# Batch 0 in finer pieces, w_tok sorted before its transposes, and batch 0's channel layer ahead of batch 1's attention

## Chip, cores, metric

One core of one Trainium2 chip. The metric is device microseconds (us) of one execution; lower is better. The kernel before: 291.4 us, median of 4 runs (290.9 to 292.0). In the profiled run the time is 1.8 us longer than the span from first to last instruction (292.5 against 290.7 for the kernel before), and positions below are us from the start of the span. Engines: PE is TensorE, DVE VectorE, ACT ScalarE, POOL GpSimd, SP the engine that issues most stores and regroupings.

## What is computed

Two stages, four batches of 768 tokens. Sizes and the parts that matter:

```
q, k, v: (4, 8 heads, 768, 64); 8 blocks of 96 tokens; P = sort_net after 5 rounds of normalising
k_sorted, v_sorted = P mixes the 8 blocks of k and of v          # per head
x = softmax(q_block @ k_sorted_block^T / 8) @ v_sorted_block      # per block, heads side by side: (4, 768, 512)
tok = w_tok @ (alpha1 * x + beta1)                                # 768 x 768, over tokens
u   = x + lam * tok
ch  = relu((alpha2 * u + beta2) @ w_ch1) @ w_ch2                  # 512 -> 2048 -> 512
out = u + lam * ch
```

## The kernel before

Batch 0 is special: nothing can overlap with it from an earlier batch, so its mixes, transposes and attention are written out by hand. From batch 1 on, a batch's attention is mixed with the channel layer (`moe_h` then `moe_ch`) of the batch before. `hf` is a half of the tokens. v of a batch is mixed into `vA`, written to a scratch tensor in HBM (`vscr`) and read back regrouped into `Vs[b % 2]`; attention of batch b cannot multiply by v before this round trip has landed.

```python
def load_weights():                    # POOL queue, in this order
    for g in range(4): pool.dma_start(W1p[... g ...], ...)
    prep_affine()                      # two POOL products: a1lB *= lamB, b1lB *= lamB
    load_raw(1, 1); load_raw(1, 0)     # v and k of batch 1
    for g in range(4): pool.dma_start(W2p[... g ...], ...)
    load_q(1)

def mix_heads(kv, h4, out, copy):      # batch 0: two heads of k or v, one copy of 128x768
    mps = psa([128, 8, 128], FT, "m_ps")
    for t6 in range(6):
        for h2 in range(2): pe.matmul(mps[... t6 ...], raw[:, h, t6, :], bigH[...])
    copy(out..., mps[:, 0:6, :]...)

def prep_wtok(which, eng):             # transposes of w_tok; token rows are 6 x 96 and 6 x 32
    for ks in which:
        pst = psb([128, S], F16, "wtok_ps")
        for tt in range(NT): pe.transpose(pst[0:96, ...],   wt16[:, tt, ks*96:(ks+1)*96], ident16[:])
        for tt in range(NT): pe.transpose(pst[96:128, ...], wt16[:, tt, TAIL+ks*32:TAIL+(ks+1)*32], ident16[:])
        eng(w_tokT[:, ks, :], pst[:])
# ... batch 0's attention (first_attention): pieces of 96 rows; blocks 6 and 7 go to a side
#     tile xs and are gathered from there into rows 96..127 of x by copies on ACT and DVE ...

    emit_attention(0, first_attention)
    # ... token matmuls, u of batch 0, a2T of half 0 ...
    moe_h(0, 0, range(3))
    mix_v(1, 1, range(3, 6), (act.copy,))
    load_raw(2, 1); load_raw(2, 0)     # raw loads of batch 2: as soon as their buffers allow
    mix_k(1)
    moe_h(0, 0, range(3, HT))
    moe_turn(0, 1)
    emit_q(1)
    for b in range(1, B):
        # ... for b > 1: q, raw loads of b + 1, mixes of b ...
        emit_attention(b)              # before the channel layer of b - 1 in the text
        if b > 1: moe_h(b - 1, 0)
        moe_ch(b - 1, 0)
        moe_h(b - 1, 1)
        moe_a(b)                       # token layer of b
        moe_ch(b - 1, 1)
```

The softmax here doesn't subtract the row's maximum and nothing guards it: scores larger than these inputs give would overflow.

## Time and profile before

| | before |
|---|---|
| time, median | 291.4 us |
| PE busy | 267.2 us of a span of 290.7 |
| token matmuls on the whole x of batch 0 start | 42.4 us |
| longest wait of PE | 9.7 us, for batch 1's regrouped v |
| start of batch 2's mixing | 125.15 us, 165.5 us before the end |

Three rows of the page of the kernel before; each digit is a fortieth of the span, in tenths of busy time or of the full clock.

```profile
PE   8689988989509999999999999999999999999992
PEclk9989999999966999999999999999999999999999
DMA  6999999999995973326936124249210133012012
```

A slice is 7.3 us. PE is nearly full, but for a hole in the eleventh and twelfth slices (5 and 0), and the low clock (the two sixes) is in the twelfth and thirteenth, in the hole's end and behind it. The chain of work that ended last names the hole (start, length, what):

```profile
23.53 3.66 PE wtok_ps L65 x48
...
42.40 1.38 PE tok_ps L65 x11
...
56.85 9.95 DMA vscr<-vA
...
67.26 19.11 DMA Vs_98<-vscr
...
86.51 1.46 PE x_ps L65 x16
...
125.15 0.13 PE rep_ps L65
...
184.59 0.13 PE rep_ps L65
```

The round trip of v took 10 + 19 us. All transfers are counted on the core's 16 DMA engines, and raw loads of batches 2 and 3 were in flight beside it. The two rep_ps lines, 59.4 us apart, are the starts of batches 2 and 3. The waits of PE (us in total, times, longest), and the two stretches at the hole:

```profile
PE x_ps L65 <- DMA Vs_98<-vscr: 9.7, 1, 9.7
```

```profile
77.00:86.50 9.50, 0.00 (x0) 0.02 (x1) 0.69 (x1) 0.00 (x0) 1.56 (x1) 0.77 1.99 145
86.50:94.50 8.00, 7.99 (x69) 4.28 (x69) 2.88 (x9) 1.61 (x2) 0.00 (x0) 0.63 0.54 116
```

The columns are the stretch, its length, busy time of PE, weight loads, DVE, ACT and POOL, then the granted clock, the DMA share (packet times added up over the 16 engines; it can pass 1 because packets overlap) and GB/s. PE does nothing for 9.5 us, and the 8 us after it run at a mean clock of 0.63.

### The profile page before, as it was taken

Reading aid. Unit: us, or ns where it says so; the run is one execution under the profiler, and the core shown is the slowest. Engines: PE = TensorE matmul, PEld = TensorE weight load, DVE = VectorE, ACT = ScalarE, POOL = GpSimd, SP = SyncE. Lnnn points to the kernel's source line nnn. Section 1 sums busy time; section 2 is a strip of 40 time slices with the busy share of each in tenths; the row PEclk is TensorE's granted clock in tenths of the full one; section 3 lists DMA queues with packets and bytes.
Section 4 is the critical chain, followed back from the end, with each engine's and each line's share of the span. In section 5 each row is a group of like instructions: output and inputs, shape, how many; then the busy total and the mean of one; then the engine's idle time right before and its main releaser. Section 6 shows DMA issues by size and latency. Waiting matters only on the chain.

```text
span 290.7 us, 5185 instructions
## 1 busy us (share of the span) xinstructions
PE 267.2 (92%) x2068; PEld 149.5 (51%) x2068; DVE 154.8 (53%) x331; ACT 130.2 (45%) x237; POOL 93.7 (32%) x100
## 2 busy tenths in 40 slices
PE   8689988989509999999999999999999999999992
PEld 3467764556214654455456644455466445645541
DVE  6856687833303939757046687670367675023032
ACT  2442497885002664058507631386076322703700
POOL 9517559716500990240042542400423600000000
PEclk9989999999966999999999999999999999999999
DMA  6999999999995973326936124249210133012012
GB/s 87 191 214 241 215 206 206 213 265 209 143 148 115 99 48 62 86 72 137 82 90 106 23 50 98 73 110 108 72 40 2 33 80 97 10 36 72 2 36 72
DMA packets 62263, 30.88 MB, mean 106 GB/s; under 512 B 48856, under 2 KB 57824, under 8 KB 62240
## 3 DMA queue, kind: packets, MB, share of 16 engines
q0 software_dynamic: 23024, 15.60, 36.5%
q1 hardware_dynamic: 39216, 14.96, 28.4%
q8 instruction: 16, 0.26, 0.4%
q14 instruction: 7, 0.06, 0.1%
HBM read 32.78 MB, written 8.65 MB: 143 GB/s over the span
## 4 chain that ended last, share of the span: by engine, by line
PE 71%; DMA 15%; ACT 5%; DVE 3%; POOL 3%; issue 1%; SPq 0%; DVEq 0%; POOLq 0%
PE ch_ps L65 27%; PE h_ps L65 24%; PE tok_ps L65 8%; DMA Vs_98<-vscr 7%; DMA wt_100<-in_moe_w_tok_dram 5%; PE x_ps L65 5%; DMA vscr<-vA 3%; PE sc_ps L65 3%; PE wtok_ps L65 2%; ACT kT L65 2%; POOL qn_82 L65 1%; PE v_ps L65 1%; ACT u_781 L65 1%; ACT vA L65 1%; ACT hTa L65 1%
## 5 line engine op out<-in xcount | busy, mean ns | idle before, releaser
L65 ACT ACTIVATE hTa<-h_ps 128x384 bf16<-128x384 f32 x96 | 45.8, 492 | 69.5 <-PE h_ps L65 68.7
L65 PE MATMUL ch_ps<-W2p,hTa 128*128 128x512 bf16 x288 | 68.7, 386 | 0.0
L65 PEld LDWEIGHTS <-W1p 128*128 128x128 bf16 x512 | 47.7, 98 | 32.4 <-issue 3.3
L65 DVE TENSOR_TENSOR ch_ps<-ch_ps,lamB 128x512 f32<-128x512 f32 x24 | 16.7, 698 | 68.6 <-PE ch_ps L65 64.2
L65 PEld LDWEIGHTS <-hTa 128*128 128x128 bf16 x288 | 28.2, 99 | 33.4 <-issue 1.1
L65 ACT ACTIVATE et<-sc_ps 96x768 f16<-96x768 f32 x32 | 24.6, 805 | 29.7 <-PE sc_ps L65 29.7
L65 PEld LDWEIGHTS <-w_tokT 128*128 128x128 f16 x198 | 16.8, 98 | 16.1 <-issue 1.3
L65 PE MATMUL ch_ps<-W2p,hTb 128*128 128x512 bf16 x96 | 24.8, 379 | 0.0
L65 PEld LDWEIGHTS <-et 96*96 96x96 f16 x256 | 16.4, 129 | 13.7 <-issue 10.5
L65 DVE TENSOR_TENSOR tok_ps<-tok_ps,a1lB 128x512 f32<-128x512 f32 x24 | 16.5, 691 | 11.1 <-PE tok_ps L65 11.1
L65 DVE CAST kT<-k_ps 64x512 f16<-64x512 f32 x24 | 16.5, 689 | 4.3 <-PE k_ps L65 4.0
L65 POOL DMA_DIRECT2D qn<-in_q_dram x12 | 10.7, 910 | 24.0 <-DMA qT<-qn 15.5
L65 DVE RECIPROCAL recip<-x_ps 96x8 f32<-96x8 f32 (+1 forms) x38 | 7.0, 188 | 21.3 <-PE x_ps L65 21.1
L65 PE MATMUL x_ps<-Vs_98,et 96*96 96x65 f16 x128 | 8.5, 216 | 9.7 <-DMA Vs_98<-vscr 9.7
L65 ACT ACTIVATE hTb<-h_ps 128x384 bf16<-128x384 f32 x32 | 15.3, 497 | 3.8 <-PE h_ps L65 3.4
L65 PEld LDWEIGHTS <-hTb 128*128 128x128 bf16 x96 | 9.3, 98 | 10.9
L65 PEld LDWEIGHTS <-kT 64*96 64x96 f16 x256 | 8.7, 124 | 10.9 <-issue 5.7
L65 PE MATMUL h_ps<-a2T_782,W1p 128*128 128x384 bf16 x64 | 11.3, 326 | 2.2 <-ACT hTa L65 1.2
L65 PE MATMUL sc_ps<-qT,kT 64*96 64x96 f16 x256 | 12.3, 217 | 0.2
L65 PE MATMUL h_ps<-a2T_2243,W1p 128*128 128x384 bf16 x64 | 12.2, 327 | 0.1
L65 PE MATMUL h_ps<-a2T_1537,W1p 128*128 128x384 bf16 x64 | 12.2, 327 | 0.1
L65 PE MATMUL h_ps<-a2T_1538,W1p 128*128 128x384 bf16 x64 | 12.1, 326 | 0.0
(265 smaller groups left out, 400.1 us busy)
## 6 DMA issues: line engine op xcount, KB each, us to landing
out_dram<-ost SPq DMA_DIRECT2D x24, 192.0 KB, 2.2
vscr<-vA SPq DMA_DIRECT2D x6, 384.0 KB, 4.6
W1p<-in_moe_w_ch_dram POOLq DMA_DIRECT2D x4, 512.0 KB, 10.5
W2p<-in_moe_w_ch_dram POOLq DMA_DIRECT2D x4, 512.0 KB, 17.2
Vs_98<-vscr SPq DMA_DIRECT2D x4, 384.0 KB, 11.5
qn<-in_q_dram POOLq DMA_DIRECT2D x12, 128.0 KB, 7.9
out_dram<-ost SPq DMA_DIRECT2D x24, 64.0 KB, 2.0
wt_100<-in_moe_w_tok_dram POOLq DMA_DIRECT2D x1, 864.0 KB, 14.7
```

The costliest lines, as they stand in the source:

```text
L65: ins = getattr(self.eng, name)(*args, **kwargs)
```

## The change

The intent: give batch 0 a finer pipeline, and fill the hole with work that is ready. `...` marks cuts.

```diff
+    spin(psb([128, 512], FT, "spin_ps")[:], 7)
     def load_weights():
         for g in range(4):
             pool.dma_start(W1p[...], ...)
-        prep_affine()
         load_raw(1, 1)
-        load_raw(1, 0)
         for g in range(4):
             pool.dma_start(W2p[...], ...)
-        load_q(1)
+            if g == 0:
+                prep_affine()
...
-    def mix_heads(kv, h4, out, copy):            # one 128x768 copy
+    def mix_heads(kv, h4, out):                  # one-bank parts, two engines
+        for lo, hi, copy in ((0, 4, dve.tensor_copy), (4, 6, act.copy)):
+            mps = psb([128, hi - lo, 128], FT, "m_ps")
...
+    def pv_tiles(h4, g, et):                     # attention of batch 0 written into full 128-row tiles
+        xps = bank[:, 0:6 * GRP].rearrange("p (a i g) -> p a i g", i=3, a=2)
+        for rows, cols, i in ((slice(0, BLK), BLK, 0), (slice(BLK, 128), 32, 3)): ...
+        dve.reciprocal(recip[:], xps[:, :, :, D])
+        dve.tensor_tensor(x_of[0][:, 3 * g:3 * g + 3, ...], xps[...], recip[...], ALU.mult)
...
+    def sort_wtok(n):                            # columns of w_tok in the order of the tiles
+        t_ = moep.tile([128, NT, 2, 128], F16, name=f"wtp_{n}", tag="a2T", bufs=3)
+        for lo, hi, base in ((0, 96, 0), (96, 128, TAIL)):
+            dve.tensor_copy(t_[:, :, :, lo:hi], wt16[...])
     def prep_wtok(which, eng):
-                pe.transpose(pst[0:96, ...], wt16[:, tt, ks * 96:(ks + 1) * 96], ident16[:])
-                pe.transpose(pst[96:128, ...], wt16[:, tt, TAIL + ks * 32:...], ident16[:])
+                pe.transpose(pst[:, tt * 128:(tt + 1) * 128], wtp[ks // 2][:, tt, ks % 2, :], ident16[:])
...
+    sc0(2, 0, 1)
+    pv0(1, 0)
+    sort_wtok(0)
+    sc0(2, 1, 1)
+    pv0(1, 1)
+    sort_wtok(1)
+    prep_wtok(range(1), dve.tensor_copy)
...
+    moe_h(0, 0, range(6))
+    mix_v(1, 1, range(4, 6), (dve.tensor_copy,))
+    pool.tensor_copy(gate[:], Vs[1][0:1, 0, 0:2])   # POOL waits for batch 1's v ...
+    load_raw(2, 1)                                  # ... before it loads batch 2
+    load_raw(2, 0)
+    moe_h(0, 0, range(6, HT))
+    moe_turn(0, 1)
+    pe.fixed = True
+    for kk in range(3):                             # channel layer of batch 0 ahead of attention 1
+        moe_ch(0, 0, (kk,))
+        mix_k(1, gs=(kk,))
+        for h4 in ((0,), (1, 2), (3,))[kk]:
+            turn_q(1, h4, dve.tensor_copy)
+    pe.fixed = False
     for b in range(1, B):
...
+            if b == 2:
+                opened = pool.tensor_copy(gate[:], Vs[0][0:1, 0, 0:2])   # a second gate, for batch 3
+                ... load_q(3); load_raw(3, 1); load_raw(3, 0) behind it ...
         emit_attention(b)
         if b > 1:
             moe_h(b - 1, 0)
-        moe_ch(b - 1, 0)
+            moe_ch(b - 1, 0)
```

Smaller parts: k and q of batch 1 are loaded after POOL has added u of batch 0; two of these six adds go to DVE; the last output tile is split into 384 and 128 columns. `spin` multiplies an identity into a PSUM tile that is overwritten later; its only use is to keep PE busy.

More of the change, by code (lines that the diff above doesn't have):

```diff
@@ L143, in load_q, with cross_q @@
             pool.dma_start(qn[:, kt, :, :], q[b].rearrange("h (p kt) d -> kt p h d", kt=NT)[kt])
+        qn_of[b] = qn
+    def cross_q(b):
         with tc.issue_after(regroup[b - 1].ins):
@@ L146, in load_q @@
                 nc.sync.dma_start_transpose(
-                    qT_of[b][:, :, kt, :], qn[:, kt, :, :].rearrange("p h d -> p (h d)")
+                    qT_of[b][:, :, kt, :], qn_of[b][:, kt, :, :].rearrange("p h d -> p (h d)")
                 )
@@ L172 @@
     lamB = const([128, C], FT, "lamB")
+    gate = const([1, 2], F16, "gate")
     ab2 = att.tile([2 * CT, 128], FT, name="ab2", tag="sel", bufs=2)
@@ L349, in mix_v, with mix_k @@
             )
-    def mix_k(b, share=(4, 0, 4)):
+    def mix_k(b, share=(4, 0, 4), gs=range(3)):
         raw = raw_of[(b, 0)]
         rhs = bigP[b][:].rearrange("p g i -> p (g i)")
-        kT = att.tile([128, H4 * NB, BLK], F16, name="kT", tag="kT", bufs=2)
-        kT_of[b] = kT
-        kv_ = kT[:].rearrange("p c (par th tp) -> p th c par tp", th=2, par=2)
-        for g in range(3):
+        if b not in kT_of:
+            kT_of[b] = att.tile([128, H4 * NB, BLK], F16, name="kT", tag="kT", bufs=2)
+        kv_ = kT_of[b][:].rearrange("p c (par th tp) -> p th c par tp", th=2, par=2)
+        for g in gs:
             kps = psa([128, 8, 128], FT, "k_ps")
@@ L371, in mix_k, with mix_k0, mix_v0 @@
                         act.copy(dst, src)
-    def mix_heads(kv, h4, out, copy):
+    def mix_heads(kv, h4, out):
         raw = raw_of[(0, kv)]
-        mps = psa([128, 8, 128], FT, "m_ps")
-        for t6 in range(6):
-            for h2 in range(2):
-                h = 2 * h4 + h2
-                pe.matmul(
-                    mps[h2 * 64:(h2 + 1) * 64, t6, :], raw[:, h, t6, :],
-                    bigH[:, h, :, :].rearrange("p i r -> p (i r)"), start=True, stop=True,
-                )
-        copy(
-            out.rearrange("p i (t r) -> p t i r", r=16),
-            mps[:, 0:6, :].rearrange("p t (i r) -> p t i r", r=16),
-        )
-    def mix_k0(h4, copy):
+        dst = out.rearrange("p i (t r) -> p t i r", r=16)
+        for lo, hi, copy in ((0, 4, dve.tensor_copy), (4, 6, act.copy)):
+            mps = psb([128, hi - lo, 128], FT, "m_ps")
+            for t6 in range(lo, hi):
+                for h2 in range(2):
+                    h = 2 * h4 + h2
+                    pe.matmul(
+                        mps[h2 * 64:(h2 + 1) * 64, t6 - lo, :], raw[:, h, t6, :],
+                        bigH[:, h, :, :].rearrange("p i r -> p (i r)"), start=True, stop=True,
+                    )
+            copy(dst[:, lo:hi], mps[:].rearrange("p t (i r) -> p t i r", r=16))
+    def mix_k0(h4):
         if 0 not in kT_of:
             kT_of[0] = att.tile([128, H4 * NB, BLK], F16, name="kT", tag="kT", bufs=2)
-        mix_heads(0, h4, kT_of[0][:, h4 * NB:(h4 + 1) * NB, :], copy)
+        mix_heads(0, h4, kT_of[0][:, h4 * NB:(h4 + 1) * NB, :])
     vT0 = []
-    def mix_v0(h4, copy):
+    def mix_v0(h4):
         vT0.append(moep.tile([128, NB, BLK], F16, name=f"vT_{h4}", tag="u32", bufs=9))
-        mix_heads(1, h4, vT0[h4][:], copy)
+        mix_heads(1, h4, vT0[h4][:])
     def turn_v0(h4, copy):
@@ L405, in turn_v0, with emit_scores, emit_pv @@
         )
-    def emit_q(b):
-        for h4 in range(H4):
-            turn_q(b, h4, dve.tensor_copy)
     x_of = {}
-    def emit_scores(b, h4):
+    def emit_scores(b, h4, g, spins=0):
         kT = kT_of[b]
         qT = qT_of[b]
-        ets = []
+        blocks = ((0, 1, 2, 6), (3, 4, 5, 7))[g] if b == 0 else range(4 * g, 4 * g + 4)
+        sps = psa([128, 2, 4, 128], FT, "sc_ps")
+        spin(sps[:, 0, :, :].rearrange("p i x -> p (i x)"), spins)
+        for ii, i in enumerate(blocks):
+            for h2 in range(2):
+                rows = slice(h2 * 64, (h2 + 1) * 64)
+                pe.matmul(
+                    sps[0:BLK, h2, ii, 0:BLK], kT[rows, h4 * NB + i, :], qT[rows, h4, :, i * 16:(i + 1) * 16],
+                    start=True, stop=True,
+                )
+        et = att.tile([BLK, 2, 4, BLK], F16, name="et", tag="et", bufs=4)
+        act.activation(
+            et[:].rearrange("p a i (r kt) -> p (a i) r kt", kt=NT),
+            sps[0:BLK].rearrange("p a i x -> p (a i) x")[:, :, 0:BLK].rearrange("p n (kt r) -> p n r kt", kt=NT),
+            AF.Exp, scale=scale,
+        )
+        return et
+    def emit_pv(b, h4, ets, x128, xs):
         for g in range(2):
-            sps = psa([128, 2, 4, 128], FT, "sc_ps")
-            if b == 0:
-                spin(sps[:, 0, :, :].rearrange("p i x -> p (i x)"), 1)
+            xps = psa([BLK, 4, 256], FT, "x_ps")
             for ii in range(4):
@@ L424, in emit_scores @@
                 for h2 in range(2):
-                    rows = slice(h2 * 64, (h2 + 1) * 64)
                     pe.matmul(
-                        sps[0:BLK, h2, ii, 0:BLK], kT[rows, h4 * NB + i, :], qT[rows, h4, :, i * 16:(i + 1) * 16],
-                        start=True, stop=True,
-                    )
-            et = att.tile([BLK, 2, 4, BLK], F16, name="et", tag="et", bufs=4)
-            act.activation(
-                et[:].rearrange("p a i (r kt) -> p (a i) r kt", kt=NT),
-                sps[0:BLK].rearrange("p a i x -> p (a i) x")[:, :, 0:BLK].rearrange("p n (kt r) -> p n r kt", kt=NT),
-                AF.Exp, scale=scale,
-            )
-            ets.append(et)
-        return ets
-    def emit_pv(b, h4, ets, x128, xs, narrow=False):
-        for g in range(4 if narrow else 2):
-            n = 2 if narrow else 4
-            if narrow:
-                bank = psb([128, 4, 128], FT, "x_ps")
-                if narrow > 1:
-                    spin(bank[:].rearrange("p a x -> p (a x)"), narrow - 1)
-                xps = bank[0:BLK].rearrange("p a x -> p (a x)")[:, 0:264].rearrange("p (i x) -> p i x", i=2)
-            else:
-                xps = psa([BLK, n, 256], FT, "x_ps")
-            for ii in range(n):
-                i = n * g + ii
-                for h2 in range(2):
-                    pe.matmul(
-                        xps[:, ii, h2 * GRP:h2 * GRP + D + 1], ets[i // 4][:, h2, i % 4, :],
+                        xps[:, ii, h2 * GRP:h2 * GRP + D + 1], ets[g][:, h2, ii, :],
                         Vs[b % NV][:, (2 * h4 + h2) * NB + i, 0:D + 1],
@@ L456, in emit_pv @@
                     )
-            recip = att.tile([BLK, n, 2], FT, name="recip", tag="recip", bufs=3)
+            recip = att.tile([BLK, 4, 2], FT, name="recip", tag="recip", bufs=3)
             sums = xps[:, :, D:D + GRP + 1:GRP]
@@ L460, in emit_pv @@
             dve.reciprocal(recip[:], sums)
-            for lo, hi in ((0, n),) if narrow or g == 0 else ((0, 2), (2, 4)):
-                i = n * g + lo
+            for lo, hi in ((0, 4),) if g == 0 else ((0, 2), (2, 4)):
+                i = 4 * g + lo
                 cols = slice(h4 * 128, (h4 + 1) * 128)
@@ L468, in emit_pv, with emit_attention @@
                 )
-    def emit_attention(b, between=None):
+    def pv_tiles(h4, g, et):
+        bank = psb([128, 4, 128], FT, "x_ps")[:].rearrange("p a x -> p (a x)")
+        xps = bank[:, 0:6 * GRP].rearrange("p (a i g) -> p a i g", i=3, a=2)
+        for rows, cols, i in ((slice(0, BLK), BLK, 0), (slice(BLK, 128), 32, 3)):
+            for h2 in range(2):
+                for ii in range(3):
+                    vi = 3 * g + ii if i == 0 else 6 + g
+                    lhsT = et[:, h2, ii, :] if i == 0 else et[:, h2, 3, 32 * ii:32 * ii + 32]
+                    pe.matmul(
+                        xps[rows, h2, ii, 0:D + 1], lhsT, Vs[0][:, (2 * h4 + h2) * NB + vi, 0:D + 1],
+                        start=True, stop=True,
+                    )
+        recip = att.tile([128, 2, 3], FT, name="recip", tag="recip0", bufs=3)
+        dve.reciprocal(recip[:], xps[:, :, :, D])
+        dve.tensor_tensor(
+            x_of[0][:, 3 * g:3 * g + 3, h4 * 128:(h4 + 1) * 128].rearrange("p i (a d) -> p a i d", d=D),
+            xps[:, :, :, 0:D], recip[:].unsqueeze(3).to_broadcast([128, 2, 3, D]), ALU.mult,
+        )
+    def emit_attention(b):
         x128 = moep.tile([128, NT, C], F16, name="x128", tag="x128", bufs=2)
@@ L473, in emit_attention, with gather @@
         x_of[b] = x128
-        def gather(lo, hi, copies=(dve.tensor_copy,) * 3):
+        def gather(lo, hi):
             for a in range(3):
-                copies[a](x128[96:128, a:a + 4:3, lo:hi], xs[32 * a:32 * a + 32, :, lo:hi])
-        def pv(h4, ets):
-            emit_pv(b, h4, ets, x128, xs, narrow=2 if between and h4 < H4 - 1 else 0)
-        if between:
-            between(pv, gather)
-            return
-        prev = emit_scores(b, 0)
+                dve.tensor_copy(x128[96:128, a:a + 4:3, lo:hi], xs[32 * a:32 * a + 32, :, lo:hi])
+        prev = [emit_scores(b, 0, g) for g in range(2)]
         for h4 in range(1, H4):
-            cur = emit_scores(b, h4)
-            pv(h4 - 1, prev)
+            cur = [emit_scores(b, h4, g) for g in range(2)]
+            emit_pv(b, h4 - 1, prev, x128, xs)
             prev = cur
@@ L491, in emit_attention @@
                 gather(0, 384)
-        pv(H4 - 1, prev)
+        emit_pv(b, H4 - 1, prev, x128, xs)
         gather(384, C)
@@ L497 @@
     rs = const([128, NT], FT, "rs")
+    wtp = []
+    def sort_wtok(n):
+        t_ = moep.tile([128, NT, 2, 128], F16, name=f"wtp_{n}", tag="a2T", bufs=3)
+        wtp.append(t_)
+        for lo, hi, base in ((0, 96, 0), (96, 128, TAIL)):
+            w = hi - lo
+            dve.tensor_copy(
+                t_[:, :, :, lo:hi],
+                wt16[:, :, base + 2 * n * w:base + (2 * n + 2) * w].rearrange("p t (k c) -> p t k c", c=w),
+            )
     def prep_wtok(which, eng):
@@ L502, in prep_wtok @@
             for tt in range(NT):
-                pe.transpose(
-                    pst[0:96, tt * 128:(tt + 1) * 128], wt16[:, tt, ks * 96:(ks + 1) * 96], ident16[:],
-                )
-            for tt in range(NT):
-                pe.transpose(
-                    pst[96:128, tt * 128:(tt + 1) * 128],
-                    wt16[:, tt, TAIL + ks * 32:TAIL + (ks + 1) * 32], ident16[:],
-                )
+                pe.transpose(pst[:, tt * 128:(tt + 1) * 128], wtp[ks // 2][:, tt, ks % 2, :], ident16[:])
             eng(w_tokT[:, ks, :], pst[:])
@@ L554, with tok_part @@
     tok_of = {}
-    def tok_part(b, kt, lo, hi):
-        if (b, kt) not in tok_of:
-            if b == 0 and kt >= 3:
-                pair = psa([128, 2, C], FT, "tok_ps")
-                for n in range(2):
-                    tok_of[(b, kt + n)] = pair[:, n, :]
-            else:
-                tok_of[(b, kt)] = psb([128, C], FT, "tok_ps")[:]
+    def tok_part(b, kt):
+        if b == 0 and kt == 3:
+            pair = psa([128, 2, C], FT, "tok_ps")
+            for n in range(2):
+                tok_of[(b, kt + n)] = pair[:, n, :]
+        elif (b, kt) not in tok_of:
+            tok_of[(b, kt)] = psb([128, C], FT, "tok_ps")[:]
         for ks in range(NT):
             pe.matmul(
-                tok_of[(b, kt)][:, lo:hi], w_tokT[:, ks, kt * 128:(kt + 1) * 128],
-                x_of[b][:, ks, lo:hi], start=(ks == 0), stop=(ks == NT - 1),
+                tok_of[(b, kt)], w_tokT[:, ks, kt * 128:(kt + 1) * 128],
+                x_of[b][:, ks, :], start=(ks == 0), stop=(ks == NT - 1),
             )
@@ L574, in moe_tok @@
                 if not done:
-                    tok_part(b, kts[n], 0, C)
+                    tok_part(b, kts[n])
                 tps = tok_of[(b, kts[n])]
@@ L637, in moe_h, with moe_ch @@
             act.activation(hT_of[(b, hf)][m], hps[:], AF.Relu)
-    def moe_ch(b, hf):
+    def moe_ch(b, hf, kks=range(3)):
         hT = hT_of[(b, hf)]
-        for kk in range(3):
+        for kk in kks:
             kt = 3 * hf + kk
-            cps = psb([128, C], FT, "ch_ps")
-            for m in range(HT):
-                pe.matmul(
-                    cps[:], hT[m][:, kk * 128:(kk + 1) * 128], W2p[:, m, :],
-                    start=(m == 0), stop=(m == HT - 1),
-                )
-            ost = att.tile([128, C], FT, name="ost", tag="ost", bufs=2)
-            dve.tensor_tensor(cps[:], cps[:], lamB[:], ALU.mult)
-            dve.tensor_tensor(ost[:], cps[:], u_of[b][kt][:], ALU.add)
-            nc.sync.dma_start(out[b, kt * 96:(kt + 1) * 96, :], ost[0:96, :])
-            nc.sync.dma_start(out[b, TAIL + kt * 32:TAIL + (kt + 1) * 32, :], ost[96:128, :])
+            last = b == B - 1 and kt == NT - 1
+            ost = att.tile([128, C], FT, name="ost", tag="ost", bufs=2)
+            for lo, hi in ((0, 384), (384, C)) if last else ((0, C),):
+                cps = psb([128, hi - lo], FT, "ch_ps")
+                for m in range(HT):
+                    pe.matmul(
+                        cps[:], hT[m][:, kk * 128:(kk + 1) * 128], W2p[:, m, lo:hi],
+                        start=(m == 0), stop=(m == HT - 1),
+                    )
+                dve.tensor_tensor(cps[:], cps[:], lamB[:, lo:hi], ALU.mult)
+                dve.tensor_tensor(ost[:, lo:hi], cps[:], u_of[b][kt][:, lo:hi], ALU.add)
+                nc.sync.dma_start(out[b, kt * 96:(kt + 1) * 96, lo:hi], ost[0:96, lo:hi])
+                nc.sync.dma_start(out[b, TAIL + kt * 32:TAIL + (kt + 1) * 32, lo:hi], ost[96:128, lo:hi])
@@ L656, with sc0, pv0 @@
+    ets = {}
+    def sc0(h4, g, spins=0):
+        ets[(h4, g)] = emit_scores(0, h4, g, spins)
+    def pv0(h4, g):
+        pv_tiles(h4, g, ets[(h4, g)])
+    x_of[0] = moep.tile([128, NT, C], F16, name="x128", tag="x128", bufs=2)
     mixing_heads()
     turn_q(0, 2, act.copy)
-    for h4 in range(H4):
-        mix_v0(h4, act.copy if h4 == 3 else dve.tensor_copy)
-        if h4 == 0:
-            turn_q(0, 3, act.copy)
+    mix_v0(0)
+    turn_q(0, 3, act.copy)
+    for h4 in range(1, H4):
+        mix_v0(h4)
@@ L662 @@
     load_weights()
-    mix_k0(0, act.copy)
+    mixing_matrices(1)
     turn_v0(0, dve.tensor_copy)
-    mix_k0(1, dve.tensor_copy)
-    def first_attention(pv, gather):
-        e0 = emit_scores(0, 0)
-        turn_v0(1, dve.tensor_copy)
-        turn_v0(2, dve.tensor_copy)
-        e1 = emit_scores(0, 1)
-        turn_v0(3, dve.tensor_copy)
-        prep_wtok(range(4), dve.tensor_copy)
-        mix_k0(2, dve.tensor_copy)
-        mix_k0(3, dve.tensor_copy)
-        prep_wtok(range(4, 6), act.copy)
-        pv(0, e0)
-        e2 = emit_scores(0, 2)
-        prep_rs()
-        prep_ab2()
-        pv(1, e1)
-        e3 = emit_scores(0, 3)
-        pv(2, e2)
-        gather(0, 256, (act.copy,) * 3)
-        moe_start(0)
-        moe_row(range(2))
-        pv(3, e3)
-        gather(256, C, (act.copy, act.copy, dve.tensor_copy))
-        for kt in range(3):
-            tok_part(0, kt, 0, 256)
-        mixing_matrices(1)
-        moe_row(range(2, NT))
@@ L694 @@
-    emit_attention(0, first_attention)
-    for kt in range(3):
-        tok_part(0, kt, 256, C)
-    for kt in range(NT):
-        moe_add(0, kt)
-    moe_tok(0, range(3), done=True)
-    for kt in range(3, NT):
-        tok_part(0, kt, 0, C)
-        mix_v(1, 1, range(kt - 3, kt - 2), (act.copy,))
+    mix_k0(0)
+    mix_k0(1)
+    turn_v0(1, dve.tensor_copy)
+    sc0(0, 0, 2)
+    sc0(0, 1, 2)
+    mix_k0(2)
+    turn_v0(2, dve.tensor_copy)
+    sc0(1, 0, 1)
+    pv0(0, 0)
+    sc0(1, 1, 1)
@@ new lines @@
+    pv0(0, 1)
+    mix_k0(3)
+    turn_v0(3, dve.tensor_copy)
+    sc0(2, 0, 1)
[5 more added lines that the diff above has]
+    prep_wtok(range(1), dve.tensor_copy)
+    sc0(3, 0)
+    pv0(2, 0)
+    prep_wtok(range(1, 2), dve.tensor_copy)
+    sort_wtok(2)
+    sc0(3, 1)
+    pv0(2, 1)
+    prep_wtok(range(2, 4), act.copy)
+    pv0(3, 0)
+    prep_wtok(range(4, 5), dve.tensor_copy)
+    prep_wtok(range(5, 6), act.copy)
+    pv0(3, 1)
+    prep_ab2()
+    prep_rs()
@@ L703 @@
+    moe_start(0)
+    moe_row(range(2, NT))
+    for kt in range(2, NT):
+        moe_add(0, kt)
+    load_raw(1, 0)
+    load_q(1)
+    for kt in range(2):
+        dve.scalar_tensor_tensor(
+            u_of[0][kt][:], b1lB[:], rs[:, kt:kt + 1], x_of[0][:, kt, :], op0=ALU.mult, op1=ALU.add
+        )
+    moe_tok(0, range(3))
+    tok_part(0, 3)
+    tok_part(0, 4)
     moe_turn(0, 0)
+    tok_part(0, 5)
+    mix_v(1, 1, range(0, 4), (dve.tensor_copy, act.copy))
     pe.fixed = act.fixed = False
-    turned = act.last
+    order = [pe.last, act.last]
@@ L709 @@
     stack = ExitStack()
-    stack.enter_context(tc.issue_after(turned.ins))
-    moe_h(0, 0, range(3))
-    mix_v(1, 1, range(3, 6), (act.copy,))
+    for eng in order:
+        stack.enter_context(tc.issue_after(eng.ins))
+    moe_h(0, 0, range(6))
+    mix_v(1, 1, range(4, 6), (dve.tensor_copy,))
+    pool.tensor_copy(gate[:], Vs[1][0:1, 0, 0:2])
     load_raw(2, 1)
@@ L715 @@
     pool.fixed = False
-    mix_k(1)
-    moe_h(0, 0, range(3, HT))
+    moe_h(0, 0, range(6, HT))
     moe_turn(0, 1)
     stack.close()
-    emit_q(1)
+    pe.fixed = True
[5 more added lines that the diff above has]
+    pe.fixed = False
     for b in range(1, B):
         if b > 1:
-            load_q(b)
-            if b + 1 < B:
-                load_raw(b + 1, 1)
-                load_raw(b + 1, 0)
+            if b > 2:
+                cross_q(b)
             mixing_matrices(b)
             mix_v(b)
+            if b == 2:
+                opened = pool.tensor_copy(gate[:], Vs[0][0:1, 0, 0:2])
+                with tc.issue_after(opened.ins):
+                    load_q(3)
+                    load_raw(3, 1)
+                    load_raw(3, 0)
             mix_k(b)
@@ L736 @@
         moe_ch(b - 1, 1)
+        if b == 1:
+            load_q(2)
+            cross_q(2)
     for hf in range(2):
```

## The prediction

> **What bounds the kernel.** The page gives PE 267.2 us busy of 290.7. In the table of stretches PE is nearly full from 95 us on, one batch every 59.4 us (rep_ps at 125.15 and 184.59 in the chain of waits). After the start of batch 2's mixing (125.15) 165.5 us follow, all PE work. What is not PE-bound lies before:
> - 0 to 44 us, batch 0. Token matmuls that need the whole x start at 42.4. w_tok lands at 23.4; then PE, DVE and ACT take turns: 72 half-width w_tok transposes (5.5 us), mixes copied by one engine (0.96 us each), x in 96-row pieces, gather copies (ACT 0.62 us each).
> - 49 to 59 us: about 2.3 us of PE waits on ACT.
> - 76.8 to 86.5 us: PE waits 9.7 us for batch 1's regrouped v (Vs_98<-vscr). vscr<-vA took 9.95 us and Vs_98<-vscr 19.1 us, beside raw loads of batches 2 and 3; in later batches the pair took about 5 and 6 to 9 us. After the gap the granted clock is 0.5 to 0.76 until 95, another 3 us. (Trainium skill, "TensorE: Matmul & The Clock Gate", Part 1: an idle window halves the clock; the trace agrees.)
>
> **The change, costed.**
> 1. Channel layers first: PE does h(0,0), 10.4 us, ch(0,0), 10.36, batch 1's k mix, 1.4, and q turns, 2.0, before attention 1 needs Vs_98. The raw loads of batches 2 and 3 are gated, so vscr and regroup should take about 5 + 8 us. vA done at about 52, Vs_98 at 65 to 68, needed at about 72: the 9.7 us stall and 3 us of slow clock go.
> 2. Batch 0: mixes in one-bank parts, DVE 128x512 (0.69) beside ACT 128x256 (about 0.4). Attention into full tiles: eight times recip (0.18) and a 128x384 multiply (about 0.55), 5.9 us, against 9.1 us plus six gather copies. Sorting w_tok adds six DVE copies; here 32x512 f16 took 0.285 and 32x768 0.353 us, about four elements a cycle (Trainium skill, "VectorE: DVE Perf Modes", perf-mode tier table, agrees), so 2.1 us in all; transposes fall from 72 to 36 (saves about 1.8 us of PE).
>  DVE now limits the front: from bigH (13.6 us) v mixes 2.8 (PE-paced, to 17.5), mixing_matrices(1) 2.5, k mixes and Vs copies 5.5, attention 5.9, sorts 2.1, w_tokT 1.7, plus waits: x whole at about 36.5.
> 3. Two of six moe_adds move to DVE; token matmuls run unsplit, 7.8 us; h(0,0) starts at about 46.5, not 50.6.
>
> **Sum.** h start 46.5; h, two turns, v parts: 59; ch, k mix, q turns: 72.5; scores and pv 5.3, h(0,1) 10.4, tok(1) 7.8, ch(0,1) 10.4: 106.5 (before 125.15). Plus 165.5, less 0.7 for the split last tile: 271.3. I add 1.5 us for unseen waits: **273 us**, range 268 to 280. Faster by over 2%: 0.94; within 2%: 0.05; slower: 0.01.
>
> **What would show it.** No Vs_98 wait in the chain; vscr and Vs_98 landings near 5 and 8 us; no slice with clock below 0.9 after 25 us; PE continuous from about 46 us; tok start near 36.5; DVE the busiest engine from 14 to 37; later batches unchanged at 59.4 us.
>
> **What would make it wrong.** Vs_98 later than 72 us (k and q loads of batch 1 still queued): PE would stall and lose its clock. DVE front slower than summed (sort copies not in the fast mode, POOL contention: 32x256 gathers went from 0.22 to 1.1 us). POOL blocked at the gate, so batch 1's u rows, or q of batch 2, arrive late. ACT crowded between 43 and 52.

## The result

282.3 us (median of 4 runs, 279.9 to 283.4), against 291.4: the ratio is 0.9675, with a 95% interval of 0.961 to 0.974. A ratio is the mean time of one kernel's fast runs over that of the other's in the same rounds, so not quite the ratio of the medians. The change is faster by about 3%. The predicted 273 us, with 268 to 280, was too low by 9 us.

The rows of the page after the change:

```profile
PE   8889599999999799999999999999999999999993
PEclk9999758999999999999999999999999999999999
DMA  6999999979999905469999143399210242012012
```

The hole in slices 11 and 12 and its slow clock are gone. A new, smaller hole stands in the fifth slice (the 5), where PE was 0.9 busy before, with a clock of 0.7, 0.5 and 0.8 in slices 5 to 7. The chain after the change:

```profile
27.16 4.18 DVE wtp_580 L65 x2
31.39 0.82 PE wtok_ps L65 x6
...
41.90 7.88 PE tok_ps L65 x30
...
53.22 3.90 PE h_ps L65 x24
...
64.72 3.45 PE ch_ps L65 x16
...
78.75 2.04 PE h_ps L65 x11
...
98.20 7.50 PE tok_ps L65 x34
105.70 10.36 PE ch_ps L65 x48
116.06 0.86 PE v_ps L65 x4
```

No Vs_98 in it: its two halves took 7.5 and 9.1 us from issues at 63.8 and 64.2, and attention 1 first reads it at 84.8. In its place stands the first sort of w_tok. The waits of PE now, and the two stretches around the new hole:

```profile
PE wtok_ps L65 <- DVE wtp_580 L65: 3.7, 1, 3.7
PE tok_ps L65 <- DVE x_1203 L65: 1.4, 2, 0.8
```

```profile
24.70:31.40 6.70, 3.03 (x51) 2.18 (x50) 6.42 (x8) 1.98 (x3) 6.70 (x9) 0.97 1.24 209
31.40:43.50 12.10, 12.10 (x142) 9.76 (x143) 7.74 (x19) 5.55 (x10) 1.85 (x3) 0.50 1.18 208
```

For 12.1 us after the wait PE is counted as busy throughout and runs at half clock. What made the sort slow? The groups of DVE by shape in the stretch from 26 to 37 us (the last columns are total us and mean ns):

```profile
L65 DVE COPY wtp_580<-wt_100 128x1152 f16<-128x1152 f16 x1 | 3.7, 3711 | 0.0
...
L65 DVE COPY wtp_657<-wt_100 128x1152 f16<-128x1152 f16 x1 | 0.5, 451 | 0.0
L65 DVE COPY wtp_611<-wt_100 128x1152 f16<-128x1152 f16 x1 | 0.5, 450 | 0.0
```

Three copies of one shape: 3711, 450 and 451 ns. The timeline of all engines at the first one:

```profile
26.14 1.12 POOL L65 DMA_DIRECT2D raw_346<-in_v_dram  x2
...
27.16 4.17 DVE L65 COPY wtp_580<-wt_100 128x1152 f16<-128x1152 f16 x2
27.21 0.82 POOL L65 DMA_DIRECT2D W2p<-in_moe_w_ch_dram  x1
28.00 1.33 POOL L65 TENSOR_TENSOR a1lB<-a1lB,lamB 128x512 f32<-128x512 f32 x1
29.23 1.31 POOL L65 TENSOR_TENSOR b1lB<-b1lB,lamB 128x512 f32<-128x512 f32 x1
30.44 2.31 POOL L65 DMA_DIRECT2D W2p<-in_moe_w_ch_dram  x3
```

The two copies of the pair are merged in the DVE line; the first lasts 3.71 us, so it ends at 30.87. POOL was never idle from 26.1, and its two products, which the change moved to this place, end at 30.54, a third of a microsecond before. The copy is of the kind that the prediction put at about four elements a cycle. The Trainium skill, page "SBUF — State Buffer", section "Who interferes with whom", says that such copies use a pair of SBUF ports that DVE shares with POOL, and that the one that comes second "fully blocks". That is the theory that the experiments test. Rivals: the first copy is slow in itself, by its strided halves or by the DMA traffic of 209 GB/s; or POOL's descriptor writing blocks it, and not the products.

### The profile page after: what moved, and what is told of

It is laid out like the page before. It is cut to its first block, busy times and chain, and to the rows that moved or that the text cites. A ratio compares the mean times of both kernels' runs of the same rounds, so it can differ in the third digit from the quotient of the medians.

```text
span 280.5 us, 5152 instructions
## 1 busy us (share of the span) xinstructions
PE 266.7 (95%) x2057; PEld 149.2 (53%) x2057; DVE 160.1 (57%) x332; ACT 126.1 (45%) x233; POOL 92.1 (33%) x100
## 4 chain that ended last, share of the span: by engine, by line
PE 85%; DVE 8%; ACT 4%; issue 1%; DMA 1%; DVEq 0%
PE ch_ps L65 29%; PE h_ps L65 27%; PE tok_ps L65 11%; PE x_ps L65 5%; PE sc_ps L65 4%; ACT kT L65 2%; PE wtok_ps L65 2%; DVE wtp_580 L65 1%; DVE x_1203 L65 1%; PE v_ps L65 1%; PE k_ps L65 1%; PE q_ps L65 1%; PE m_ps L65 1%; ACT et L65 1%; PE vt_ps L65 1%
## 5 line engine op out<-in xcount | busy, mean ns | idle before, releaser
L65 ACT ACTIVATE hTa<-h_ps 128x384 bf16<-128x384 f32 x96 | 46.1, 493 | 52.3 <-PE h_ps L65 51.4
L65 PE MATMUL ch_ps<-W2p,hTa 128*128 128x512 bf16 (+2 forms) x300 | 66.6, 371 | 0.0
L65 DVE TENSOR_TENSOR ch_ps<-ch_ps,lamB 128x512 f32<-128x512 f32 (+2 forms) x25 | 16.9, 675 | 63.8 <-PE ch_ps L65 61.1
L65 PEld LDWEIGHTS <-w_tokT 128*128 128x128 f16 x180 | 15.2, 101 | 18.9 <-issue 2.9
L65 PE MATMUL ch_ps<-W2p,hTb 128*128 128x512 bf16 (+2 forms) x100 | 25.0, 370 | 0.0
L65 PEld LDWEIGHTS <-et 96*96 96x96 f16 (+1 forms) x288 | 17.5, 128 | 3.5 <-issue 0.4
L65 DVE RECIPROCAL recip<-x_ps 96x8 f32<-96x8 f32 (+1 forms) x32 | 6.2, 196 | 14.5 <-PE x_ps L65 14.1
L65 PE MATMUL h_ps<-a2T_800,W1p 128*128 128x384 bf16 x64 | 12.9, 327 | 0.0
L65 PE MATMUL h_ps<-a2T_2219,W1p 128*128 128x384 bf16 x64 | 12.2, 327 | 0.1
L65 PE MATMUL h_ps<-a2T_2220,W1p 128*128 128x384 bf16 x64 | 12.1, 326 | 0.0
L65 PE MATMUL h_ps<-a2T_1504,W1p 128*128 128x384 bf16 x64 | 11.7, 327 | 0.0
L65 PE MATMUL h_ps<-a2T_1505,W1p 128*128 128x384 bf16 x64 | 11.6, 326 | 0.0
L65 PE MATMUL x_ps<-Vs_96,et 96*96 96x65 f16 (+1 forms) x160 | 11.4, 222 | 0.0
```

Of the source, the lines that this page charges most:

```text
L65: ins = getattr(self.eng, name)(*args, **kwargs)
```

## The experiments

Eleven kernels, all correct, in three sets. Each set shared its runs of the kernel before (291.4, 292.2, 292.2 us medians). Times are medians of all 4 runs; ratios are to the kernel before. The changed kernel was not run again in these sets, and the kernel before differed by 0.8 us between them, so a difference of about 1 us from the changed kernel says nothing. Three of the 44 runs were over 1.5% above the fastest of their kernel (the profiled one of the first experiment, 279.65 us, among them); such runs are classed slow and are not in the ratios.

| kernel | us | ratio | clocks of the 4 runs |
|---|---|---|---|
| changed | 282.3 | 0.968 | 0.966 to 0.986 |
| POOL products later | 275.9 | 0.945 | 0.975 to 1.0 |
| first sort on ACT | 278.2 | 0.953 | 0.982 to 0.994 |
| spins in the wait | 277.4 | 0.951 | 0.997 to 1.0 |
| products later and spins | 275.5 | 0.944 | 0.992 to 1.0 |
| no sort | 276.5 | 0.946 | 0.996 to 1.0 |
| batch 0 of before, rest changed | 283.3 | 0.973 | 0.984 to 0.992 |
| batch 0 changed, rest of before | 294.2 | 1.005 | 0.948 to 0.969 |
| no gates | 287.6 | 0.983 | 0.958 to 0.975 |
| gates, channel layer not ahead | 279.6 | 0.957 | 0.978 to 0.987 |
| one row held for attention 1 | 278.0 | 0.952 | 0.973 to 0.985 |
| products later, spins, row held | 273.4 | 0.935 | 0.999 to 1.0 |

### The cause of the slow sort

**POOL products later.** They wait for a part of w_tokT:

```diff
-            if g == 0:
-                prep_affine()
...
     prep_wtok(range(2, 4), act.copy)
+    pool.tensor_copy(gate[:], w_tokT[0:1, 2, 0:2])
+    prep_affine()
     pv0(3, 0)
```

> Edit: only the two GpSimd products (a1lB, b1lB) move, from beside the first w_tok sort copy to behind w_tokT part 2. My theory (the 128x1152 sort copy took 3.71 us, against 0.45 for its twins, because GpSimd held the shared SBUF ports with the two products): the copy falls to at most 1.5 us, PE's wait of 3.67 us for wtp to at most 1.3, the clock no longer drops to 0.5 between 31 and 43 us, the token matmuls start at 36 to 37.5 instead of 41.8, time 5 to 6.5 us below the changed kernel. Rival 1 (the copy is slow by itself, its first use or its strided halves, or because of the DMA traffic of 206 GB/s): it stays at 3.5 us or more and so does the time. Rival 2 (descriptor writing by GpSimd blocks it as well): 2 to 3 us, time 2 us lower.

DVE and then POOL in the profiled run (which was one of the slow runs, 279.65 us; the copy's length is DVE's and POOL's matter, not the clock of PE):

```profile
27.14 1.30 DVE L65 COPY wtp<-wt 128x1152 f16<-128x1152 f16 x2
```

```profile
25.72 1.12 POOL L65 DMA_DIRECT2D raw<-in_v_dram  x2
26.78 1.58 POOL L65 DMA_DIRECT2D W2p<-in_moe_w_ch_dram  x2
...
34.86 1.25 POOL L65 TENSOR_TENSOR a1lB<-a1lB,lamB 128x512 f32<-128x512 f32 x1
```

The pair falls from 4.2 us to 1.3 with descriptor writing still beside it, and PE waits 0.8 us for it instead of 3.7. So the products were the cause of most of it; rival 1 is out, and of rival 2 about 0.7 us is left in this run (1.3 against the 0.6 of an undisturbed pair). In the changed kernel rival 2 has a part too: at its own 0.45 us the copy would have ended at 27.6, but the first product began only at 28.00, and until then POOL was writing descriptors. The time fell by 6.4 us (medians of all four runs). One part of what was expected failed: in this run the clock still fell, as the stretches show, without a wait of that length.

```profile
25.00:30.00 5.00, 4.20 (x65) 3.05 (x63) 4.68 (x11) 1.85 (x4) 4.10 (x6) 0.87 1.23 205
30.00:35.00 5.00, 5.00 (x57) 4.33 (x57) 3.01 (x8) 2.56 (x4) 1.03 (x3) 0.50 1.26 211
35.00:40.00 5.00, 5.00 (x71) 3.89 (x70) 2.82 (x7) 2.29 (x6) 2.35 (x3) 0.50 1.08 207
```

The same program had a clock of 1.0 in two of its four runs (274.2 and 274.5 us), and 0.986 and 0.975 in the others (277.3 and 279.7). So a wait of 3.7 us is not needed for the clock to fall; what decides it in this stretch stays open (see the end of the next chapter).

**First sort on ACT.** ACT has its own ports by the same page.

```diff
-    sort_wtok(0)
+    sort_wtok(0, act.copy)
```

> Edit: only the first sort pair goes to ACT, which was idle 27.97 to 32.8. My theory (ports shared by DVE and GpSimd): the pair takes about 1.7 us on ACT, undisturbed by GpSimd; PE waits under 1.5 us for wtp, the clock stays at 1, token matmuls start at 36.5 to 38, time 4 to 6 us below the changed kernel; the DVE copies of the second sort now meet GpSimd's products instead and may take 1 to 2.5 us. Rival (slow source or DMA traffic): the ACT copy is slow too, 3 us or more, and nothing is gained.

The pair took 1.14 + 0.51 us on ACT beside POOL's work, and PE waited 0.45 us for it: the strided source is not slow to read in itself. The second pair, on DVE, then met the products, as expected, and PE waited 1.1 us for what stood behind it. DVE, then POOL:

```profile
28.35 3.21 DVE L65 COPY wtp<-wt 128x1152 f16<-128x1152 f16 x2
```

```profile
28.25 1.29 POOL L65 TENSOR_TENSOR a1lB<-a1lB,lamB 128x512 f32<-128x512 f32 x1
29.48 1.28 POOL L65 TENSOR_TENSOR b1lB<-b1lB,lamB 128x512 f32<-128x512 f32 x1
```

Its first copy took 2.74 us, so it ended at 31.09, 0.33 us after the second product (30.76). In the changed kernel the same distance was 0.33, and in the next experiment, where again the second pair was hit (3.08 us from 28.45), it was 0.33. Three more experiments below show the same 0.33: the one with a row held at the first pair (3.43 us), and "no gates" and "gates, channel layer not ahead" at the second (2.87 us each, while their first pair took its normal 0.62). These two have the front of the changed kernel, word for word, so which pair is hit depends on small shifts in POOL's queue, and neither the first use nor the place of a copy makes it slow. Whichever copy meets the products ends right behind them: the cause is settled. Time 278.2, 4.0 us below the changed kernel.

**Spins in the wait.** Nothing else is edited.

```diff
     sort_wtok(1)
+    spin(psb([128, 512], FT, "spin_ps")[:], 17)
     prep_wtok(range(1), dve.tensor_copy)
```

> Edit: 17 idle 512-column matmuls fill PE's wait for the first sorted w_tok; the slow copy stays. If the loss is mostly the clock that the wait costs (12 us at 0.5): copy still 3.7 us, clock 1.0 from 31 to 43, token matmuls start at 37.5 to 39 instead of 41.8, time 3 to 4.5 us lower. If the loss is the wait itself: time within 1 us of the changed kernel.

The first w_tok transpose started at 31.3, as late as in the changed kernel (31.4), but the token matmuls at 38.2 instead of 41.8, and all four runs lie between 277.2 and 277.4 with a clock of 0.997 or more. So 4.9 us of the loss was the slow clock: here the transposes start as late as in the changed kernel, but at full clock. The gain is in kind what was expected (3 to 4.5 us), and slightly more. But the copy was not the expected 3.7 us. In the profiled run the products missed the first pair and hit the second, and the late start comes from the spins themselves (DVE, then PE):

```profile
27.15 0.66 DVE L65 COPY wtp<-wt 128x1152 f16<-128x1152 f16 x2
...
28.45 3.56 DVE L65 COPY wtp<-wt 128x1152 f16<-128x1152 f16 x2
```

```profile
27.64 3.84 PE L65 MATMUL spin_ps<-ident 128*128 128x512 f16 x17
```

PE has no listed wait for a sort copy in this run. So it measures a late start at full clock; it does not measure the slow first copy at full clock.

**Both mends:** the products later, and nine spins (six before the first w_tok transposes, one and two before the last two scores of batch 0).

> The two mends together: GpSimd's products moved behind w_tokT as in the first experiment, and nine idle matmuls around the sort (six before the first w_tok transposes, one and two before the last scores). Both losses are then gone: sort copy at most 1.5 us, clock 1.0 from 20 to 60 us in every run, token matmuls start at 35.5 to 37, time 272.5 to 275, and all runs within 1 us of each other (the first experiment's ranged from 274.2 with a clock of 1.0 to 279.7 with 0.975). If the clock falls for another reason than a lack of array work, the spread stays.

275.5 us, runs 275.3 to 276.3: the spread is gone, as expected, the median 0.5 us above the expected range. The two stretches that were shown for the changed kernel:

```profile
24.70:31.40 6.70, 6.70 (x93) 4.37 (x92) 5.33 (x15) 2.68 (x4) 4.85 (x7) 1.00 1.23 206
31.40:43.50 12.10, 12.10 (x149) 8.07 (x149) 8.90 (x18) 8.04 (x14) 9.47 (x9) 1.00 1.18 209
```

The token matmuls start at 36.2 and h(0,0) at 46.1; the prediction had 36.5 and 46.5. The spins are not free: the two runs with the products later and without spins that kept their clock were 1.0 to 1.3 us faster than this median.

**No sort.** The changed kernel with the 72 half-width transposes of before.

```diff
-    sort_wtok(0)      # and (1), (2)
-                pe.transpose(pst[:, ...], wtp[ks // 2][:, tt, ks % 2, :], ident16[:])
+                pe.transpose(pst[0:96, ...], wt16[...], ident16[:])       # and 96:128
```

> The changed kernel without the sort: 72 half-width transposes straight from the loaded w_tok, no sort copies on DVE. If the sort costs more than it saves as the change placed it: no wait for wtp, clock 1.0 from 25 to 45 us, token matmuls start at 37 to 39 instead of 41.8, time 276 to 279. If sorting is worth its price even so: time at or above the changed kernel's 282.

276.5 us, four runs within 0.3, token matmuls at 37.3: as expected, 5.7 us faster than the changed kernel. As the change placed it, the sort cost far more than it saved. Without disturbance it may be worth 1 to 2 us (275.5 with both mends, 274.2 and 274.5 in the two full-clock runs with the products later, against 276.5); these kernels differ in more than the sort, and the intervals of the first pair overlap, so that is not shown.

### Which part brought the gain

**Batch 0 of before, the rest changed.** Built from the kernel before: its batch 0, with the changed order of loads, gates and channel layer.

> Batch 0 as before the change (no sorting, wide mixes, narrow attention pieces), everything from the first channel layer on as after it. My theory: the whole gain comes from the new order behind batch 0 (no wait for Vs_98, no slow clock), and the new batch 0 costs time as it stands: h(0,0) starts at 49 to 51 us against 53.2, time 278 to 281, 1 to 4 us below the changed kernel. Rival (the finer batch 0 carries a good part of the gain): time 285 or more.

283.3 us: between the two expected ranges, so neither is right as stated. The part behind batch 0 alone brings 8.1 of the 9.1 us. So the finer batch 0 is worth about 1 us as the change placed it, which is within the noise; mended, it is worth almost 8 (275.5 with both mends against 283.3). This kernel has small waits of its own: h(0,0) starts at 51.4 us, PE waits 1.0 us there for a2T, and 1.6 us more for batch 2's v mix around 117 us.

**Batch 0 changed, the rest of before.** The changed kernel with the old order of loads, no gates, and attention 1 ahead of the channel layer.

> Batch 0 as changed (sorted w_tok, finer mixes), everything from the first channel layer on as before the change: attention 1 ahead of the channel layer, raw loads of batches 2 and 3 not held back. My theory (the whole gain comes from the order behind batch 0): PE again waits 8 to 14 us for Vs_98 and its clock falls after it, time 288 to 294, within 2% of the kernel before. Rival (the finer batch 0 carries half the gain): 284 to 287.

294.2 us, no gain, but not for the reason I gave: PE waited only 2.0 us for the regrouped v. It waited 6.6 us for k of batch 1, which the scheduler had put ahead of batch 0's transposes in PE's order, and v itself was mixed only by 67 us. Its sort was hit as well (PE waited 3.0 us for it). The combination brought a wait of its own, so it shows that the finer batch 0, as it stood, gains nothing in the old surroundings, and says little of why.

**No gates.**

```diff
-    pool.tensor_copy(gate[:], Vs[1][0:1, 0, 0:2])
...
-                opened = pool.tensor_copy(gate[:], Vs[0][0:1, 0, 0:2])
-                with tc.issue_after(opened.ins):
+                (the three loads of batch 3 ungated)
```

> The changed kernel with both GpSimd gates removed, so that raw loads of batches 2 and 3 and q of batch 3 start as soon as their buffers allow. If the gates matter: the regroup into Vs_98 takes 15 us or more again, lands later than 84.8 us, where attention 1 first reads it, and PE waits; time 2 us or more above the changed kernel. If the order alone is enough: Vs_98 lands before 84.8 even beside these loads (before the change the pair took 29 us from 57, that is 86 here), PE waits at most 2 us and the time is within 2 us.

287.6 us, or 286.7 for the three fast runs (the fourth, 294.3, is a slow one): by the ratios, 0.983 against 0.968, about 4.5 us above the changed kernel. The gates matter, but again the wait is another than expected: Vs_98 took up to 14.7 us and still landed in time, at 79.7 before the first read at 87.3. The loss is 4.8 us in which PE waits for a PSUM tile that DVE cannot empty, because its store buffers are held by output stores, and a clock of 0.65 and 0.67 from 80 to 85 and to 90 us. The last of these stores took 5.8 us to land; the first was issued only at 72.1, because issuing the regroup ahead of it took SP 7.1 us instead of 2.1. A long landing alone is not enough: in the changed kernel two stores took 7.9 and 8.8 us and PE did not wait. Lastly, there are 1.9 us in which u of batch 1 waits for POOL, busy with loading q.

**Gates, channel layer not ahead.**

```diff
-        moe_ch(0, 0, (kk,))
...
         emit_attention(b)
         if b > 1:
             moe_h(b - 1, 0)
-            moe_ch(b - 1, 0)
+        moe_ch(b - 1, 0)
```

> The changed kernel with the gates and its order of loads kept, but ch(0,0) emitted after attention 1 again, as before the change. If the gates alone had removed the wait (Vs_98 landed by 71.8 us in the changed kernel, and without ch(0,0) PE would first read it at about 70): PE waits at most 2 us for it, time within 1.5 us of the changed kernel. If the order of PE is needed too: a wait of 3 us or more for Vs_98, slow clock behind it, time 3 us or more above.

279.6 us, with no wait of PE for Vs_98 at all; it reads it first at 77.3. So putting the whole channel layer ahead was not needed to close the hole. The gates were not needed for it either: without them, with the channel layer ahead, no wait for Vs_98 came (the experiment before this one). Either was enough; k and q of batch 1 loaded late are common to both and were not tested alone. The time is 2.6 us below the changed kernel, though the intervals of the two ratios overlap; part of that is the next point (h(0,1) is followed by no wait for x here), part the clock of the sort stretch, which differs from run to run.

**One row held for attention 1.** After attention 1, PE of the changed kernel waits 1.4 us for x of batch 1: h(0,1) is used up by then.

```diff
     for kk in range(3):
-        moe_ch(0, 0, (kk,))
+        if kk < 2:
+            moe_ch(0, 0, (kk,))
...
         if b > 1:
             moe_h(b - 1, 0)
             moe_ch(b - 1, 0)
+        else:
+            moe_ch(0, 0, (2,))
```

> The changed kernel with the third output row of ch(0,0) emitted after attention 1 and no longer fixed in PE's order. My theory (the 1.4 us that PE waits for x of batch 1 before its token matmuls come from a lack of other work, h(0,1) being used up): the wait goes, time 1 to 2 us lower. Rival (the scheduler puts the row elsewhere, or DVE, which copies the gathered rows, is what limits there): same within 0.5 us.

278.0 us, 4.3 lower, more than the 1 to 2 expected. The token matmuls of batch 1 run without a gap (PE's timeline):

```profile
88.53 5.37 PE L65 MATMUL h_ps<-a2T,W1p 128*128 128x384 bf16 x32
93.73 7.93 PE L65 MATMUL tok_ps<-x,w_tokT 128*128 128x512 f16 x36
```

From the start of h(0,0) to the end of ch(0,1) it takes 60.6 us (51.3 to 111.9) instead of 62.8 (53.1 to 115.9), so the row is worth 2.2 us. The other 2 us lie before h(0,0), where nothing was edited: the clock of the sort stretch again (low for 10.2 us in this profile, 13.7 in that of the changed kernel).

**All together:** products later, spins, row held.

> Mended changed kernel (GpSimd products later, nine idle matmuls) with, in addition, the third row of ch(0,0) kept back for attention 1. If the two gains add (275.5 less the 1.4 us that PE waits for x of batch 1): 273.5 to 274.5, no PE wait over 0.5 us between 20 and 110 us, clock 1.0. If they don't: 275 to 276.

273.4 us, all four runs between 273.3 and 273.5, as expected. No wait of PE over 0.3 us is listed after 20 us, and the page shows a full clock:

```profile
PE   8889999999999999999999999999999999999993
PEclk9999999999999999999999999999999999999999
```

It beats both kernels: 0.935 of the kernel before, 8.9 us below the changed one.

## Why the prediction was wrong

The sum of the prediction, boundary by boundary (us from the start of the span; starts from PE's timeline and the chain):

| boundary | predicted | changed | both mends | mends and row |
|---|---|---|---|---|
| token matmuls of batch 0 start | 36.5 | 41.8 | 36.2 | 36.3 |
| h(0,0) starts | 46.5 | 53.1 | 46.1 | 46.2 |
| ch(0,0), k mix and q turns end | 72.5 | 78.7 | 71.7 | in other order |
| ch(0,1) ends | 106.5 | 116 | 108.9 | 106.9 |
| span ends | 271.3 | 280.5 | 273.5 | 271.7 |

**The step that failed** is in the second item of the costs: "2.1 us in all" for the six sort copies, and with it "x whole at about 36.5" and "no slice with clock below 0.9 after 25 us". The copies took 5.9 us (3.71 + 0.54, 0.45 + 0.52, 0.45 + 0.25). The copy rate was right: 0.45 us for 1152 elements, twice, as the tier table of the Trainium skill's page "VectorE: DVE Perf Modes" and this trace had it. What I left out was POOL. The text named the danger ("POOL contention: 32x256 gathers went from 0.22 to 1.1 us") but no term of the sum carried it, though the diff shows the two products moving to exactly this place in POOL's queue. The delay of 3.6 us at the first pair became 6.6 us at the start of h(0,0), because it came with more than 12 us of half clock; the spins experiment, with the transposes starting as late, got 4.9 us back.

**The second, smaller miss:** from 72.5 to 106.5 I added up scores, products, h(0,1), tok(1) and ch(0,1) as if PE were never short of work: 34.0 us. It took 37.3 in the changed kernel (78.7 to 116), and 37.2 with both mends. Attention's own latency needs more filling than h(0,1) has: 1.4 us is the wait for x of batch 1, and holding back one row of ch(0,0) recovered 2.2 us. Most of the rest is a term that was set too low: scores and products with h(0,1) kept PE from 78.7 to 95.9, which leaves them about 6.8 us beside h's 10.4, not 5.3.

**Right in outcome, other in cause:** the wait for Vs_98 and the slow clock behind it went, as predicted, and the two transfers took about 5 and 8 to 9 us as predicted. The headline "channel layers first" is not shown to have done it: with the gates and the order of loads alone the wait was gone too, and with the channel layer ahead and no gates as well. vA was ready at 58.7 instead of 52 and Vs_98 came later than the predicted 65 to 68, but the first read moved as well, to 84.8, so none of it cost time. With the mends these landed near the prediction (vscr issued at 51.8, the gate behind Vs_98 open at 65.3).

**Not confirmed:** DVE as the limit of the front. With the mends PE, spins included, is busy without a break from 20 us to 45, and DVE has gaps. mixing_matrices(1), put at 2.5 us, took 1.0 (0.21 + 0.22 + 0.29 + 0.28): the two products with two SBUF inputs that had taken 1.03 and 1.25 us beside POOL's adds met an idle POOL engine this time. That is consistent with the same sharing of ports, with no experiment on it.

**Small:** I set the time equal to the span, which is 1.8 us shorter; the 1.5 us added for unseen waits hid that. The split last tile saved what was expected: from the end of batch 1's part to the end of the span 164.4 us against 165.5 less 0.7.

**Open:** what decides whether the clock falls in the sort stretch when PE has no long wait. It fell in two of four runs of one program. Thin array work is my reading, and the spins, which add 512-column matmuls, do stop it; but a count of array activity is not in the profile. A rival is idle time: in every profiled run whose clock fell in this stretch, PE had stood idle for at least 0.7 us of the 3.4 us before the fall (0.8 in the run with the products later), and in the unsorted and the mended runs it was busy for all of 20 to 40 us. But 0.7 us of idle time between 17.2 and 20.6 brought no fall, so that is not the whole rule either.

## What to carry to other kernels

Before moving an instruction on POOL, look at what DVE runs at that moment: a fast DVE copy from SBUF to SBUF beside two POOL products took eight times its own time here, and a cost for such a copy is incomplete without POOL's timeline beside it. Price a delay together with the clock that it can take along: about half of the 9 us lost here was PE at half speed afterwards, and a few idle matmuls kept the clock and removed the spread between runs. When a wait for a transfer ends, test the order of transfers and the order of compute apart; here either alone was enough to end it, so the credit cannot go to the reordering alone.

## What the Trainium skill lacked or had wrong

- "SBUF — State Buffer", section "Who interferes with whom": it says who blocks whom, and the runs agree (a copy of 0.45 us took 2.74 to 3.71 us), and that the one that issues first gets the ports. It does not say how a waiting DVE copy fares against several POOL instructions in a row. Here the copy issued at 27.16, while POOL was writing descriptors (one write to 27.27, the next from 27.21 to 28.04) and before the products at 28.00 and 29.23, and finished 0.33 us behind the last product: it got in at none of the boundaries. Six runs show the 0.33.
- The same section: descriptor writing by POOL alone, beside the same pair of copies, cost about 0.7 us in one run (1.30 against 0.62). No page gives a size for that direction.
- "TensorE: Matmul & The Clock Gate", Part 1, ties the fall to an idle window of about 3.4 us and the return to about 3.4 us of sustained work; it also tells of a kernel in which frequent short idles did it. In the run with the products later the clock was 0.50 from 30 to 40 us although PE's longest wait from 20 us on was 0.8 us, and in the changed kernel it stayed at 0.50 for 12.1 us in which the profile counts PE as busy without a break. Part 4 says that transposes do not count as busy in the same way, and w_tok's are part of this stretch. That does not explain it all: the unsorted kernel, with 72 of them, held a clock of 1.00 from 26.8 to 37.0 us, and in the run with a row held the clock was back at 39.8 after only transposes and attention matmuls (the token matmuls began at 41.4). No page has a threshold for small matmuls, and none comes out of these runs.
